# Softmax denominators written into a score bank of the next head pair

## Chip, cores and metric

The kernel runs on one core of one Trainium2 chip. The metric is the device time of one execution in microseconds. TensorE (PE) does matmuls and transposes, VectorE (DVE), ScalarE (ACT) and GpSimd (POOL) the rest, SyncE (SP) issues the DMAs. All of them run their own instruction lists in order and wait for each other by semaphores.

## What is computed

Attention with 4 sink keys and a window of 128 keys, for 4 batches of 8 heads with 768 queries of 64 numbers, and behind it a two-layer feed-forward net (512 to 2048 to 512, leaky ReLU) on the 3072 rows:

```python
scores = scale * np.matmul(q, k.transpose(0, 1, 3, 2))
keep = is_sink | in_window
scores = np.where(keep, scores, -1000000000.0)
scores = scores - np.max(scores, axis=-1, keepdims=True)
a = np.exp(scores)
a = a / (np.sum(a, axis=-1, keepdims=True) + 1e-09)
attn_out = np.matmul(a, v)
...
h = x @ w_in
g = np.maximum(0.01 * h, h)
return (g @ w_out).astype(np.float32)
```

All in float32. The feed-forward products are done in three passes on split operands.

## The kernel before

The work is cut into 8 units of 384 queries (half a batch), each of 4 pairs of heads and 3 query tiles (j = 0, 1, 2). A unit's attention gives the x of its feed-forward part, and one unit's feed-forward matmuls (16 steps, lines 549 and 586) are interleaved by hand on PE with the next unit's attention. Unit 0 has nothing to be interleaved with: its attention runs alone at the start of the program, with short dummy matmuls (line 272) between its transposes.

In units 0 and 1 ("native") one query tile of one pair goes as follows. PE computes the scores of the two heads into two PSUM banks (line 296; the two heads use different halves of PE's rows). DVE masks a bank and takes the row maximum (line 308), ACT does the exponential and the row sum into `sm` (line 310), POOL copies out the sink columns (line 458). Two tiles later PE transposes the result (line 337) and ACT (in pair 0 of unit 0: DVE) copies it to `pt` (line 342). When all three tiles of a pair are done, `spread` makes the reciprocals of the six row sums: DVE adds 1e-9 and writes the six numbers into columns of a score bank that the scores leave free (line 320, to `SPARE`, column 264 and up), takes the reciprocal from there back to `sm` (line 321), and POOL widens it to `rb` (line 324). `gather`, three tiles behind the pair's last one (two for the last pair of unit 0), transposes the sink columns and `rb` on PE (lines 372, 375) and copies them to `r` (line 379). `values`, one tile later, multiplies `pt` by the values (line 392) and the sinks (line 398), and DVE scales the result with `r` (line 404), which also frees the PSUM bank for a later transpose.

The score banks go round: four of them in unit 0 (tags s0, s1, o0, o1), two in unit 1 and later. A new score tile in a bank waits until the last instruction that reads or writes the old tile is done, and `spread`'s two DVE instructions count among these, since they use the bank's free columns. PE's order is written by hand (`attention_stream` with its lags, and `mlp_stream`). The orders on DVE, ACT, POOL and SP are set by a scheduler from the order in which the code emits the work. The same DVE also decodes the weights from 64-bit to 32-bit numbers (lines 185, 187, 189), and ACT and POOL split them (lines 198, 199); these lie between the attention's instructions all through units 0 and 1.

Of the kernel before, what the change touches and what calls it, by code (L numbers as in the profile page):

```python
# [147 lines left out]
def fast_path(ctx, tc, cpool, qp, qk, vu, vs, vt, wq, out, ident, lims, wz, negm, wmin, wmax):  # L148
# [68 lines left out]
    def native(u):  # L217
        return u < NATU

    def load_pair(u, pair):  # L220
        b, half = divmod(u, 2)
        n = TU + NK[half]
        raw = apool.tile([P, TU + NK[1]], F32, tag="qksp", name=f"qkn{u}_{pair}")
        nc.sync.dma_start(out=raw[:, 0:n], in_=qp[half][pair])
        raws[u, pair] = raw

    def load_values(u, pair):
        b, half = divmod(u, 2)
        vr = apool.tile([P, 4 * P], F32, tag="v", name=f"v{u}_{pair}")
        nc.sync.dma_start(out=vr[:, 0:NVB[half] * P], in_=vu[half][b, pair])  # L230
        vraws[u, pair] = vr

    def load_head(u, h):
        b, half = divmod(u, 2)
        n = TU + NK[half]
        raw = iopool.tile([P, TU + NK[1]], F32, tag="raw", name=f"qkraw{u}_{h}", bufs=3)
        nc.sync.dma_start(out=raw[:, 0:n], in_=qk[half][b, h])
        raws[u, h] = raw

    def load_sinks(u, pair):  # L240
        if native(u):
            sv = apool.tile([SKR, TU], F32, tag="sv", name=f"sv{u}_{pair}")
            nc.sync.dma_start(out=sv[0:SKN, :], in_=vs[u // 2, pair])
            svs[u, pair] = sv
            return
        raw = xpool.tile([SKR, TU], F32, tag="rb", name=f"svr{u}_{pair}", bufs=1)[:, 0:P]
        nc.sync.dma_start(out=raw, in_=vt[u // 2, pair])
        svs[u, pair] = raw
# [56 lines left out]
    def soft(u, h, j, w, src, mask, sm):  # L305
        col = (u * H + h) * T + j
        neg = negm[:, col:col + 1]
        anchor[0] = nc.vector.tensor_tensor_reduce(out=w, in0=src, in1=mask, scale=-SCALE, scalar=3.0e38,  # L308
                                                   op0=ALU.add, op1=ALU.min, accum_out=neg)
        nc.scalar.activation(out=w, in_=w, func=AF.Exp, scale=-1.0, bias=neg, accum_out=sm)  # L310
# [6 lines left out]
    def spread(u, pair, state, ps):  # L317
        sm = state["sm"]
        rest = ps[:, SPARE:SPARE + 2 * T].rearrange("p (j h) -> p j h", j=T)
        nc.vector.tensor_scalar(out=rest, in0=sm, scalar1=1e-9, scalar2=None, op0=ALU.add)  # L320
        nc.vector.reciprocal(out=sm, in_=rest)
        rb = xpool.tile([P, TU], F32, tag="rb", name=f"rb{u}_{pair}", bufs=1)
        rb = rb.rearrange("p (c d) -> p c d", c=2 * T)
        nc.gpsimd.tensor_copy(out=rb, in_=sm.rearrange("p j h -> p (j h)").rearrange("p (c o) -> p c o", o=1)
                              .broadcast_to([P, 2 * T, D]))
        state["rb"] = rb
# [89 lines left out]
    def ahead(u, pair):  # L416
        return (u, pair + 1) if pair < NPAIR - 1 else (u + 1, 0)

    count = [0]

    def attend(u, pair, pend):
        state = {"sk": sks[pair % 2]}
        nxt = ahead(u, pair)

        def later(lag, f, join=False):
            pend.append((count[0] + lag, f, join))

        def fetch(o):
            more = nxt[0] < NU
            if native(u) and native(nxt[0]) and nxt not in raws:  # L430
                load_pair(*nxt)
            if more and o == 0:
                load_values(*nxt)
            if not native(u) and o == 0:
                load_head(u, 2 * pair + 1)
            elif more and not native(nxt[0]):
                load_head(nxt[0], 2 * nxt[1])

        def tile_pt():
            if "pt" not in state:  # L440
                state["pt"] = apool.tile([P, 2, 2 * TU], F32, tag="pt", name=f"pt{u}_{pair}", bufs=1)

        def pt_then(f, *args):
            tile_pt()
            f(*args)

        if native(u):
            state["sm"] = apool.tile([P, T, 2], F32, tag="sm", name=f"sm{u}_{pair}")
            sp = raws.pop((u, pair))
            for j in range(T):  # L450
                kn = KSL[u % 2][j][1]
                pss = scores(u, pair, j, (0, 1), sp)
                w = apool.tile([P, 2, W3], F32, tag="pk", name=f"pk{u}_{pair}_{j}", bufs=3)
                a = P if kn == W3 else 0
                for o, ps in enumerate(pss):
                    soft(u, 2 * pair + o, j, w[:, o, 0:kn], ps[:, 0:kn], masks[min(T * (u % 2) + j, 2)],
                         state["sm"][:, j, o:o + 1])
                    nc.gpsimd.tensor_copy(out=state["sk"][:, 0, j, o, :], in_=w[:, o, a:a + NSK])
                if j == 0:
                    fetch(0)  # L460
                    if native(nxt[0]):
                        load_sinks(*nxt)
                    if u == 0 and pair == 0:
                        rest(anchor[0])
                    if u == 0 and pair == 2:
                        whole_lim.append(whole_limits(tc, cpool, lim_raw, lim_lo, anchor[0]))
                        late.append(late_masks(tc, cpool, iopool, masks, anchor[0]))
                count[0] += 1
                if j == T - 1:
                    spread(u, pair, state, pss[1])  # L470
                later(LAGT, lambda j=j, w=w: pt_then(turn_native, u, pair, j, w, state))
                yield
        else:
            for o in range(2):
                h = 2 * pair + o
                sp = split_head(u, h)
                fetch(o)
                (split_sinks if o else load_sinks)(u, pair)
                w = apool.tile([P, 2 * W3], F32, tag="pk", name=f"pk{u}_{h}", bufs=3)
                w = w[:, 0:T * W1].rearrange("p (j k) -> p j k", j=T)  # L480
                sm = apool.tile([P, T], F32, tag="sm", name=f"sm{u}_{h}")
                for j in range(T):
                    ps, = scores(u, pair, j, (o,), sp)
                    if KSL[u % 2][j][1] == W3:
                        nc.vector.copy_predicated(out=ps[:, W1:W3], mask=late[0][1], data=ps[:, 0:P])  # L485
                        src = ps[:, P:W3]
                    else:
                        src = ps[:, 0:W1]
                    soft(u, h, j, w[:, j], src, late[0][0][min(T * (u % 2) + j, 2)], sm[:, j:j + 1])
                    count[0] += 1  # L490
                    if j == T - 1:
                        nc.vector.tensor_scalar(out=sm, in0=sm, scalar1=1e-9, scalar2=None, op0=ALU.add)
                        nc.vector.reciprocal(out=sm, in_=sm)
                        nc.vector.tensor_tensor(out=w, in0=w, in1=sm.rearrange("p (j o) -> p j o", o=1)
                                                .broadcast_to([P, T, W1]), op=ALU.mult)
                        sk, sinks = state["sk"], w[:, :, 0:NSK]
                        nc.gpsimd.tensor_copy(out=sk[:, 0:3:2, 0:T, o, :].bitcast(F32R),
                                              in_=sinks.rearrange("p (r j) s -> p r j s", r=1)
                                              .broadcast_to([P, 2, T, NSK]))
                        nc.gpsimd.tensor_tensor(out=sk[:, 1, 0:T, o, :], in0=sinks, in1=sk[:, 0, 0:T, o, :],  # L500
                                                op=ALU.subtract)
                        later(LAGT, lambda o=o, w=w: pt_then(turn_packed, u, pair, o, w, state))
                    yield
        last = u == 0 and pair == NPAIR - 1
        if native(u):
            later(LAGT if last else LAGG, lambda: gather(u, pair, state))
        later(LAGT if last else LAGV if native(u) else LAGP, lambda: values(u, pair, state), not native(u))
# [125 lines left out]
    for x, _ in enumerate(mlp_stream()):  # L633
        u, r = divmod(x, mlp_steps)
# [216 lines left out]
```

## Time and profile before

| | |
|---|---|
| median of 3 runs | 702.59 us (701.48 to 704.52) |
| the profiled execution | 702.91 us, of which its span is 701.1 us |
| busy: PE, DVE, ACT, POOL | 98%, 64%, 45%, 46% of the span |
| granted TensorE clock, mean | 0.999 |

The span runs from the first to the last instruction; 1.8 us lie around it. PE is busy all the time but for the first 37 us or so, in which unit 0's attention runs alone, and for a few waits behind that. An engine that sits idle costs nothing unless PE waits for it.

### The profile page before, as it was taken

To read this page: it belongs to the slowest core of one execution; us is meant where nothing else is said; L and a number is where in the kernel's file an instruction comes from. 1 tells how busy PE (TensorE), PEld (TensorE's weight loads), DVE (VectorE), ACT (ScalarE), POOL (GpSimd) and SP (SyncE) were. 2 spreads that over 40 slices of the span, in tenths; PEclk is the share of its full clock that TensorE was granted. 3 is DMA by queue.
4 is the path that set the end of the run, shared out by engine and by line. 5 is a ranking of instruction groups with operands and counts; after the bars stand their busy time and mean duration, and the time that the engine had idled before them with its cause. 6 is when DMAs were issued, how large, how long until landed. Compare 5 with 4: busy or idle time off the path is not lost.

```text
span 701.1 us, 11524 instructions
## 1 busy us (share of the span) xinstructions
PE 687.3 (98%) x3950; PEld 597.8 (85%) x3950; DVE 446.1 (64%) x1183; ACT 318.8 (45%) x827; POOL 321.0 (46%) x442
## 2 busy tenths in 40 slices
PE   8899999999999999999999999999999999999996
PEld 5577788988888988888898888888888889889995
DVE  5997887655656665565566565556566565377772
ACT  4865566444454444444444444444444444222221
POOL 4676688544444543543444454354344444122220
PEclk9999999999999999999999999999999999999999
DMA  6666556222123111222113221221222320068751
GB/s 223 207 223 197 192 204 202 82 66 69 47 72 108 56 43 61 60 85 69 58 53 106 70 57 47 62 91 44 67 73 53 110 74 33 1 218 277 252 169 48
DMA packets 29535, 74.14 MB, mean 106 GB/s; under 512 B 3488, under 2 KB 9120, under 8 KB 29472
## 3 DMA queue, kind: packets, MB, share of 16 engines
q1 hardware_dynamic: 29184, 73.10, 32.0%
q8 instruction: 32, 0.52, 0.3%
q14 instruction: 31, 0.25, 0.1%
q10 hardware_dynamic: 288, 0.26, 0.1%
HBM read 67.06 MB, written 6.29 MB: 105 GB/s over the span
## 4 chain that ended last, share of the span: by engine, by line
PE 93%; DVE 3%; DMA 1%; ACT 1%; issue 0%; SPq 0%; ACTq 0%; DVEq 0%
PE h L549 38%; PE o L586 37%; PE acc L392 6%; PE s L301 5%; PE t L348 3%; PE s L296 2%; PE t L337 1%; DVE pk L308 1%; DMA qkraw<-in_qk 1%; PE acc L398 1%; DMA qkn<-in_qp 1%; PE acc L388 1%; PE t L350 0%; ACT pk L310 0%; DVE ob L599 0%
## 5 line engine op out<-in xcount | busy, mean ns | idle before, releaser
L568 POOL TENSOR_TENSOR gl<-g,gh 128x384 fp32r<-128x384 f32 x127 | 129.9, 1023 | 276.2 <-ACT gh L567 260.8
L549 PE MATMUL h<-xh,wih 128*128 128x384 f32 x512 | 180.8, 353 | 0.0
L549 PE MATMUL h<-xl,wih 128*128 128x384 f32 x512 | 172.7, 337 | 0.0
L549 PE MATMUL h<-xh,wil 128*128 128x384 f32 x512 | 172.7, 337 | 0.0
L586 PE MATMUL o<-woh,gh 128*128 128x512 f32 (+1 forms) x400 | 153.5, 385 | 0.2 <-DVE ob L599 0.2
L586 PE MATMUL o<-wol,gh 128*128 128x512 f32 (+1 forms) x400 | 152.8, 385 | 0.0
L310 ACT ACTIVATE pk<-pk,negm 128x132 f32<-128x132 f32 (+1 forms) x192 | 81.6, 426 | 96.7 <-DVE negm L308 96.3
L559 ACT ACTIVATE g<-h 128x384 f32<-128x384 f32 x127 | 62.0, 488 | 123.7 <-PE h L549 103.4
L586 PE MATMUL o<-woh,gl 128*128 128x512 f32 (+1 forms) x400 | 113.8, 387 | 0.0
L549 PEld LDWEIGHTS h<-xh,wih 128*128 128x128 f32 x512 | 96.4, 188 | 4.0 <-issue 2.2
L549 PEld LDWEIGHTS h<-xl,wih 128*128 128x128 f32 x512 | 96.6, 189 | 0.4 <-POOL xl L406 0.2
L549 PEld LDWEIGHTS h<-xh,wil 128*128 128x128 f32 x512 | 96.1, 188 | 0.0
L567 ACT CAST gh<-g 128x384 fp32r<-128x384 f32 x128 | 65.7, 513 | 65.4 <-DVE g L566 64.8
L566 DVE TENSOR_TENSOR g<-h,g 128x384 f32<-128x384 f32 x127 | 69.9, 550 | 35.0 <-ACT g L559 34.9
L586 PEld LDWEIGHTS o<-woh,gl 128*128 128x128 f32 x400 | 74.0, 188 | 17.1 <-POOL gl L568 0.4
L586 PEld LDWEIGHTS o<-woh,gh 128*128 128x128 f32 x400 | 75.1, 188 | 12.0 <-DVE ob L599 0.9
L586 PEld LDWEIGHTS o<-wol,gh 128*128 128x128 f32 x400 | 75.1, 188 | 11.0
L485 DVE COPY_PREDICATED s<-tri,s 128x128 f32<-128x128 int8 x120 | 35.0, 292 | 53.8 <-PE s L301 51.9
L262 POOL TENSOR_TENSOR qksp<-qkraw,qksp 64x396 fp32r<-64x396 f32 (+1 forms) x48 | 56.4, 1176 | 23.1 <-POOL gl L568 18.6
L301 PEld LDWEIGHTS s<-qksp 128*128 128x128 f32 x288 | 53.5, 188 | 8.6
L301 PE MATMUL s<-qksp 128*128 128x260 f32 (+1 forms) x288 | 56.3, 277 | 0.0
L261 ACT CAST qksp<-qkraw 128x780 fp32r<-128x780 f32 (+1 forms) x48 | 43.2, 901 | 25.2 <-PE s L301 22.2
(114 smaller groups left out, 853.8 us busy)
## 6 DMA issues: line engine op xcount, KB each, us to landing
craw<-in_wq SPq DMA_DIRECT2D x32, 512.0 KB, 4.1
qkraw<-in_qk SPq DMA_DIRECT2D x24, 454.0 KB, 3.2
qkraw<-in_qk SPq DMA_DIRECT2D x24, 390.0 KB, 3.0
wiraw<-in_wq SPq DMA_DIRECT2D x16, 512.0 KB, 4.2
woraw<-in_wq SPq DMA_DIRECT2D x16, 512.0 KB, 3.7
out<-ob SPq DMA_DIRECT2D x23, 256.0 KB, 2.0
v<-in_vu SPq DMA_DIRECT2D x16, 256.0 KB, 2.6
v<-in_vu SPq DMA_DIRECT2D x16, 192.0 KB, 2.4
```

The source lines that it names most:

```text
L261: nc.scalar.copy(out=sp[:, 0:TU + n], in_=raw[:, 0:TU + n])
L262: nc.gpsimd.tensor_tensor(out=sp[D:P, TU:TU + n], in0=raw[D:P, TU:TU + n], in1=sp[D:P, TU:TU + n].bitcast(F32), op=ALU.subtract)
L301: nc.tensor.matmul(pss[0][:, 0:kn], lhsT=sp[:, off + j * P:off + (j + 1) * P], rhs=sp[:, TU + k0:TU + k0 + kn], start=c == 0, stop=c == 1)
L310: nc.scalar.activation(out=w, in_=w, func=AF.Exp, scale=-1.0, bias=neg, accum_out=sm)
L392: nc.tensor.matmul(acc[o * D:(o + 1) * D, qo:qo + m], lhsT=vv[:, kb * P + o * D:kb * P + (o + 1) * D], rhs=state["pt"][:, o, po:po + m], s ...
L485: nc.vector.copy_predicated(out=ps[:, W1:W3], mask=late[0][1], data=ps[:, 0:P])
L549: nc.tensor.matmul(ph[:, 0:TU], lhsT=w[:, cs], rhs=x, start=cc == 0 and c == 0, stop=cc == NCC - 1 and c == 2)
L559: nc.scalar.mul(g, ph[:, 0:TU], 0.01)
L566: anchor[0] = nc.vector.tensor_tensor(out=g, in0=ph[:, 0:TU], in1=g, op=ALU.max)
L567: nc.scalar.copy(out=gh, in_=g)
L568: (nc.vector if step == NU * NFC - 1 else nc.gpsimd).tensor_tensor(out=gl, in0=g, in1=gh.bitcast(F32), op=ALU.subtract)
L586: nc.tensor.matmul(acc, lhsT=(gl if c == 2 else gh)[:, t * P:(t + 1) * P], rhs=(wl if c == 1 else wh)[:, cols], start=f == 0 and c == 0, s ...
```

## The change

`spread` of a pair is not emitted behind the pair's own last tile. It is kept in a list and emitted behind the two heads' line 308, 310 and 458 of the next pair's first tile, and the bank whose free columns it uses is that tile's second bank (`pss[1]`), not the second bank of the pair's own last tile. For the last pair of unit 1 it is the first bank of unit 2 (the second branch). Nothing is added or left out.

```diff
@@ in fast_path, ahead of attend @@
     count = [0]
+    waiting = []
...
@@ attend, units 0 and 1, in the loop over j @@
                 if j == 0:
+                    if waiting:
+                        waiting.pop()(pss[1])
                     fetch(0)
...
                 count[0] += 1
                 if j == T - 1:
-                    spread(u, pair, state, pss[1])
+                    waiting.append(lambda ps: spread(u, pair, state, ps))
...
@@ attend, the other units @@
                     soft(u, h, j, w[:, j], src, late[0][0][min(T * (u % 2) + j, 2)], sm[:, j:j + 1])
+                    if waiting:
+                        waiting.pop()(ps)
```

PE's order stays as it is. On the other engines the scheduler arranges the instructions anew. In the rows below, `s_5_0` is head 5's score bank of tile 0, and the number behind it only tells tiles of one name apart; `m` are masks, `di` and `wi` a weight being decoded, `lim` a small constant.

DVE, where pair 2 of unit 0 begins (the rows with `negm` alone read out the row maximum). Before:

```order
L185 TENSOR_SCALAR di_302<-wiraw_206 128x512
L107 SCALAR_TENSOR_TENSOR lim_hi<-lim_lo,lim_hi 128x2
L308 ISA pk_2_1_350,negm<-s_4_1_346,m_95 128x260
L308 ISA negm 128x1
L187 SCALAR_TENSOR_TENSOR di_302<-wiraw_206,di_302 128x512
L108 SCALAR_TENSOR_TENSOR lim<-lim_hi,lim_lo 128x2
L308 ISA pk_2_1_350,negm<-s_5_1_347,m_95 128x260
```

The same place now:

```order
L185 TENSOR_SCALAR di_302<-wiraw_206 128x512
L320 TENSOR_SCALAR s_5_0_255<-sm_1_184 128x6
L107 SCALAR_TENSOR_TENSOR lim_hi<-lim_lo,lim_hi 128x2
L308 ISA pk_2_1_350,negm<-s_4_1_346,m_95 128x260
L308 ISA negm 128x1
L187 SCALAR_TENSOR_TENSOR di_302<-wiraw_206,di_302 128x512
L308 ISA pk_2_1_350,negm<-s_5_1_347,m_95 128x260
L308 ISA negm 128x1
L321 RECIPROCAL sm_1_184<-s_5_0_255 128x6
L108 SCALAR_TENSOR_TENSOR lim<-lim_hi,lim_lo 128x2
```

Pair 1's lines 320 and 321, which stood ahead of line 404 of pair 0, have come behind it, line 321 behind both heads' line 308 of tile 1; they use bank `s_5_0`, which `s_5_2` needs next.

DVE, where unit 1 begins. Before:

```order
L320 TENSOR_SCALAR s_7_2_472<-sm_3_386 128x6
L321 RECIPROCAL sm_3_386<-s_7_2_472 128x6
L404 TENSOR_TENSOR r_2_491<-acc_2_520,r_2_491 128x384
L308 ISA pk_0_0_498,negm<-s_0_0_494,m_96 128x260
L308 ISA negm 128x1
L308 ISA pk_0_0_498,negm<-s_1_0_495,m_96 128x260
```

And now, from the last of these rows on:

```order
L308 ISA pk_0_0_494,negm<-s_1_0_491,m_96 128x260
L308 ISA negm 128x1
L185 TENSOR_SCALAR di_516<-wiraw_511 128x512
L320 TENSOR_SCALAR s_1_0_491<-sm_3_382 128x6
L308 ISA pk_0_1_555,negm<-s_0_1_551,m_96 128x260
L308 ISA negm 128x1
L187 SCALAR_TENSOR_TENSOR di_516<-wiraw_511,di_516 128x512
L321 RECIPROCAL sm_3_382<-s_1_0_491 128x6
```

Line 321 of pair 3 has moved behind unit 1's first bank of tile 1 and two weight steps, and the bank it uses, `s_1_0`, is the one of two that `s_1_1` needs next.

ACT, in pair 3 of unit 0. Before:

```order
L310 ACTIVATE pk_3_1_457,sm_3_386<-pk_3_1_457,negm 128x260 x2
L198 CAST wih_445<-wi_408 128x512
L379 COPY r_2_491<-sk_2_486 128x512
L310 ACTIVATE pk_3_2_475,sm_3_386<-pk_3_2_475,negm 128x260 x2
L198 CAST woh_449<-wo_413 128x512
```

And now:

```order
L310 ACTIVATE pk_3_1_457,sm_3_382<-pk_3_1_457,negm 128x260 x2
L198 CAST wih_445<-wi_408 128x512
L310 ACTIVATE pk_3_2_475,sm_3_382<-pk_3_2_475,negm 128x260 x2
L379 COPY r_2_487<-sk_2_482 128x512
L198 CAST woh_449<-wo_413 128x512
```

The copy of pair 2's gathered rows to `r` stands behind two exponentials that it stood ahead of.

## Rows read from the trace of the kernel before

**Rows 1.** Stretches: us, busy us of PE, PEld, DVE, ACT, POOL; clock, DMA, GB/s

```profile
9.50:36.70 27.20, 24.02 (x169) 14.97 (x168) 22.76 (x78) 19.89 (x63) 15.70 (x39) 1.00 0.60 203
40.00:60.00 20.00, 20.00 (x115) 15.34 (x113) 19.34 (x43) 12.97 (x32) 16.28 (x20) 1.00 0.69 220
36.70:700.50 663.80, 655.28 (x3743) 577.67 (x3741) 419.08 (x1083) 295.14 (x753) 300.22 (x376) 1.00 0.31 100
```

**Rows 2.** PE's waits in the first 30 us: us in total, times, longest

```profile
PE t L337 <- DVE r L404: 1.3, 2, 1.0
PE s L296 <- DVE sm L321: 0.9, 1, 0.9
```

**Rows 3.** Timeline, pair 1 of unit 0: start, us, engine, line, [idle before <-releaser]

```profile
9.54 0.70 PE L296 MATMUL s<-qkn 64*128 64x260 f32 x2
...
10.93 0.20 DVE L321 RECIPROCAL sm<-s 128x6 f32<-128x6 f32 x1
...
11.18 0.70 PE L296 MATMUL s<-qkn 64*128 64x260 f32 x2 [0.95 <-DVE sm L321]
11.82 0.66 PE L337 MATMUL t<-ident,pk 128*128 128x128 f32 x4
...
12.51 0.71 PE L296 MATMUL s<-qkn 64*128 64x260 f32 x4
...
13.74 0.30 PEld L296 LDWEIGHTS s<-qkn 64*128 64x128 f32 x4 [0.17 <-DMA qkn<-in_qp]
```

**Rows 4.** Timeline, pair 2 of unit 0

```profile
18.14 1.00 POOL L406 TENSOR_TENSOR xl<-r,xh 128x384 fp32r<-128x384 f32 x1
...
18.28 0.87 DVE L107 SCALAR_TENSOR_TENSOR lim_hi<-lim_lo,lim_hi 128x2 f32<-128x2 f32 x1
...
18.85 0.71 PE L296 MATMUL s<-qkn 64*128 64x260 f32 x4
...
20.02 0.15 DVE L108 SCALAR_TENSOR_TENSOR lim<-lim_hi,lim_lo 128x2 f32<-128x2 f32 x1
...
22.22 0.71 PE L398 MATMUL acc<-r,sv 32*128 32x128 f32 x4
```

**Rows 5.** Groups from 9 to 37 us: count | busy us, mean ns | idle before

```profile
L310 ACT ACTIVATE pk<-pk,negm 128x260 f32<-128x260 f32 x18 | 9.1, 509 | 3.3 <-DVE negm L308 3.1
...
L308 DVE CUSTOM_DVE_ANT_0 pk<-s,m 128x260 f32<-128x260 f32 x16 | 6.4, 422 | 1.4 <-PE s L296 1.3
...
L404 DVE TENSOR_TENSOR r<-acc,r 128x384 f32<-128x384 f32 x4 | 2.2, 545 | 2.4 <-PE acc L398 2.4
L187 DVE SCALAR_TENSOR_TENSOR di<-wiraw,di 128x512 int32<-128x512 int32 x3 | 2.1, 691 | 0.0
...
L324 POOL COPY rb<-sm 128x384 f32<-128x384 f32 x4 | 2.0, 505 | 0.9 <-PE t L337 0.4 <-PE acc L392 0.3 <-DVE sm L321 0.2
...
L379 ACT COPY r<-sk 128x512 f32<-128x512 f32 x3 | 1.7, 578 | 0.0
```

**Rows 6.** Timeline of PE, pairs 2 and 3 of unit 0 to the first h

```profile
24.46 0.66 PE L337 MATMUL t<-ident,pk 128*128 128x128 f32 x4 [1.05 <-DVE r L404]
...
31.07 0.66 PE L337 MATMUL t<-ident,pk 128*128 128x128 f32 x4 [0.30 <-DVE r L404]
...
31.77 0.71 PE L296 MATMUL s<-qkn 64*128 64x260 f32 x4
...
34.22 1.30 PE L392 MATMUL acc<-pt,v 128*64 128x256 f32 x12 [0.61 <-ACT pt L342]
...
36.73 0.44 PE L549 MATMUL h<-xh,wih 128*128 128x384 f32 x1
```

**Rows 7.** Timeline, unit 1, tiles 0 and 1 of pair 2

```profile
64.30 0.43 DVE L308 CUSTOM_DVE_ANT_0 pk<-s,m 128x260 f32<-128x260 f32 x1 [1.39 <-PE t L337]
64.65 0.42 DVE L308 CUSTOM_DVE_ANT_0 pk<-s,m 128x260 f32<-128x260 f32 x1
...
67.10 0.71 PE L296 MATMUL s<-qkn 64*128 64x260 f32 x4
```

## Prediction

> **What bounds the kernel now.** I read the stretches first: from 36.7 us to the end PE is busy 655.28 of 663.80 us, and the clock is 1.00 throughout [rows 1]. So behind 36.7 us nothing but PE's own work counts, and what the change can do it does by moving the first `h` matmul, at 36.73 [rows 6], and with it all that follows. Ahead of it PE is idle for about 3 of 27.2 us [rows 1]. The waits of PE come next: in the first 30 us it waits 0.9 us for line 321 and 1.3 us for line 404 [rows 2]. The first of these is the wait that the change is about: `s_3_1` (second head, tile 1 of pair 1) needs the bank of `s_1_2`, which pair 0's denominators hold until line 321 has ended at 11.13; it starts at 11.18 [rows 3]. It happens in one pair of the seven of units 0 and 1 that have one behind them. In the others the bank came free long before its next use.
>
> **Rules of the walk**, all from rows: a hand-over between engines takes 0.05 us (10.93 + 0.20 to 11.18), PE's next instruction starts about 0.06 before the end of the one ahead (11.18 + 0.70 to 11.82) [rows 3], DVE's about 0.08 before (64.30 + 0.43 to 64.65) [rows 7], unless it reads what that one wrote. The two heads' scores use different halves of PE's rows: both together take 0.71 us, one alone 0.70 [rows 3]. **So a wait that catches only the second head costs the wait and some 0.64 us more.** The added and removed instructions cancel: lines 320, 321 and 324 run as often as before; everything is in where they stand.
>
> **Pair 1: a gain that a transfer takes back.** `s_3_1` no longer waits, both heads go at 9.54, and the transpose behind them at 10.18 in place of 11.82 [rows 3]: 1.64 us gained. `s_2_2` follows 0.69 later, at 10.87 (11.82 to 12.51 before). But the denominators now sit in `s_3_0`, which `s_3_2` needs: DVE does line 320 and `s_3_1`'s line 308 and comes to line 321 at about 11.2, so `s_3_2` starts at 11.5 and ends its turn at 12.15. The gather (0.59 us) brings PE to 12.74. There it needs `qkn` of pair 2, whose transfer held it until 13.74 already, by 0.17 us [rows 3]; that transfer was issued much earlier and does not move. Gain: 0.
>
> **Pair 2: the new wait.** PE is unchanged up to `s_4_2` at 18.85 [rows 4]. On DVE line 320 slips in at about 18.3, ahead of line 107. Line 107 took 0.87 us and ended at 19.15, as POOL's line 406 ended (18.14 + 1.00); line 108, the same kind on as small a tile, took 0.15 [rows 4]. So line 107 waits for POOL, and line 320 hides in that. Line 308 of `s_5_1` takes line 108's place at 20.02, line 321 follows 0.35 later [rows 7], 20.37 to 20.57, and `s_5_2` can start at 20.62. `s_4_2` has run alone; PE gets on at 20.62 + 0.64 = 21.26, not at 19.49: 1.77 later. The copy to `rb` (0.51 [rows 5]) ends at 21.13 and is covered by that wait. Gather, `s_6_0` and `s_7_0` (0.59 + 0.42) and line 392 (1.30 less 0.06) bring line 398 to 23.50, against 22.22 [rows 4]: 1.28 later, since of the 1.77 a wait of 0.49 falls away, in which `s_7_0` stood for `s_5_1`'s line 308 (18.85 + 0.64 + 0.59 + 0.42 + 1.24 is 21.74, not 22.22). DVE has its weight steps done by about 23.9 and takes line 404 at 24.24, ends it at 24.79 (0.545 [rows 5]), and the transpose that needs its bank starts at 24.85. Before it stood there until 24.46, having waited 1.05 us for line 404 behind DVE's queue [rows 6]. So 0.39 is left of 1.28.
>
> A rule speaks against this place. The Trainium skill, page "SBUF — State Buffer", section "SBUF: two separate sides", says that VectorE and GpSimd share a pair of ports that one instruction holds to its end while the other is shut out, an instruction of VectorE with two inputs in SBUF being one that needs it. Line 107's 0.87 us agrees. By it the `rb` copy, which now comes right behind line 321, could shut out line 108 for 0.5 us; DVE would be free at 24.4 and the sum 0.2 larger. I leave it out, as line 108 starts about 0.1 us ahead of the copy.
>
> **Pair 3.** From line 404 at 24.24 DVE needs 2.24 us to line 321 (0.47, twice 0.22 for the narrow line 308, 0.61 each for lines 185 and 187, which is 0.69 less the overlap [rows 5], 0.12 for line 320): 26.48 to 26.66. PE, from 24.85, comes to `s_7_2` at 26.88. In time by 0.2 us, no wait. But on ACT the copy to `r` (line 379) now stands behind the two exponentials of tile 2 (0.51 each), the second of which can end at 29.97 only; the copy takes 0.58 [rows 5], so line 398 starts at 30.6 where PE is there at 29.97. Line 404 ends at 31.85 and the transpose behind it starts at 31.9, not at 31.07 [rows 6]: 0.83 later.
>
> **Unit 1, tiles 0 and 1.** Line 404 starts at 31.30, line 308 of the two banks of tile 0 at 31.74 and 32.09, line 185 at 32.44, line 320 at 33.04. Then stands line 308 of `s_0_1`, which PE runs alone from 32.60 to 33.30; then line 187 at 33.68 and line 321 from 34.28 to 34.46. Only two banks go round here, so `s_1_1` needs that one: it starts at 34.51, and the next transpose at 35.15, where before both heads went at 31.77 [rows 6] and it at 32.41. 2.74 later. `rb`, on POOL from about 34.5, is in time for the gather at 35.8. Line 342 then copies the transposes (35.85 to 36.42) and line 392 starts at 36.47, not at 34.22: 2.25 later, since 0.5 of the old wait of 0.61 [rows 6] is taken up. Behind it nothing waits, and the first `h` comes at 38.98 in place of 36.73.
>
> **In units 1 and 2** the new place is covered: in the tightest of the pairs, pair 2, line 308 of the second bank is at 64.65 [rows 7], lines 185, 320, 187 follow, line 321 would end at about 66.5, and the bank is wanted at 67.10 [rows 7]. If that cover is gone the cost is the lateness and 0.64.
>
> **The sum.** 0 + 0.39 + 0.44 + 1.42 = 2.25 us, on a span of 701.1: 703.35, and 705.16 for the execution with the 1.81 around it. The profiled execution was 0.32 above the median of 702.59, so the median becomes **704.8**. Bounds of the sum: if DVE kept the times of before up to pair 3's line 404, line 321 would still come a microsecond later than `s_1_1` is wanted, and the first `h` 1.1 us later: 703.7. If the 0.5 absorbed at 34.22 is not there and pair 3's margin of 0.2 fails: 2.25 + 0.5 + 0.3, 705.6.
>
> **Rivals.**
> 1. *The gain stays.* `qkn` lands earlier than the row shows, or the freed wait lets DVE run ahead so that none of the new places is late. For it: 1.64 us come free at 10.2 and DVE has nothing to do there. Against it: the transfer's wait at 13.74 [rows 3]. If all of the waits of [rows 2] go, 2.2 us: 700.4; if the new ones eat most of it, 702.6 to 703.
> 2. *Unit 1's two banks (slower).* Between 40 and 60 us DVE is busy 19.34 of 20 us and PE all of it [rows 1]. There line 321 holds a bank of two while DVE's queue is full. It decides from a lateness of 0.6 us on at 67.10 [rows 7]. At 2 us late that place costs 1.4 + 0.64, and PE has no idle time there to take it up: 702.6 + 2.25 + 2.0 = 706.9. Against it: DVE has 1.39 us of idle just ahead [rows 7], so its queue starts empty.
> 3. *The clock.* PE's pauses grow to about 1.3 us, twice. In the rows a pause of 1.05 us left the granted clock at 1.00 [rows 1, 6], its upper level of 2.4 GHz. If one of the new ones took it to 1.2 GHz, PE's work of 24.02 us in 27.2 [rows 1] would run at half speed in part: a quarter of it is 6 us, 708.6 or above. The Trainium skill, page "TensorE: Matmul & The Clock Gate", section "Part 1: The HAM clock gate", says that idleness halves the clock; no row here shows it.
> 4. *Nothing happens:* the wait for line 321 is only renamed and every new place is covered, 702.6. The order on DVE speaks against it.
>
> **How the numbers follow.** A measurement of this kernel can tell about 0.5% (3.5 us) from no change; 699.1 and 706.1 are the borders. My forecast, 0.58, with a range of 703.5 to 706.0. Rival 1, 0.15, and rival 4, 0.08, both mostly within 0.5%, with 0.03 of them faster. Rival 2, 0.14, and rival 3, 0.03, slower; 0.02 for other losses. A little of rival 2 stays within 0.5%. That gives faster 0.03, same 0.79, slower 0.18. The range of 701.8 to 706.9 takes in the forecast, rival 4, the upper half of rival 1 and the lower half of rival 2.
>
> **What would show it.** Right: PE's wait for line 321 ahead of `s_3_1` gone, and PE still waiting for `qkn` until about 13.7; new waits for line 321 of about 1 us at 20 to 21 us and at 33 to 35 us, each with one head's scores alone ahead of it; the first `h` near 39; behind it the same idle times as before. Wrong: the first `h` at or ahead of 36.7 (rival 1 or 4), waits of `s` for line 321 behind 40 us (rival 2), a granted clock below 1.00 in the first 40 us (rival 3).

## The result and the profile after

The changed kernel takes 709.02 us (707.67 to 709.51, 5 executions), against 702.59 (701.48 to 704.52) before: a ratio of 1.0079, 95% interval 1.0055 to 1.0103. The ratios here and below are worked out over the fast executions and are not quotients of two medians (709.02 by 702.59 is 1.0091); one execution of the kernel before, of 1356.57 us, counts nowhere. It is slower by 0.8%, where I had forecast 704.8 and at most 706.9. The profiled execution took 709.15 us, a span of 707.4 and 1.75 around it. The span is 6.3 us longer than the one of before.

The stretches come first again. These answer to [rows 1], with the same columns (us, busy us of PE, PEld, DVE, ACT, POOL; clock, DMA, GB/s):

```profile
9.50:41.70 32.20, 28.43 (x169) 17.19 (x168) 22.86 (x79) 20.40 (x64) 16.64 (x39) 0.88 0.52 184
20.00:24.00 4.00, 4.00 (x22) 2.47 (x21) 2.75 (x6) 2.66 (x7) 2.26 (x6) 0.57 0.68 234
36.90:43.90 7.00, 6.87 (x28) 4.83 (x28) 3.07 (x8) 2.74 (x9) 2.31 (x5) 0.52 0.48 162
41.70:706.80 665.10, 656.45 (x3743) 578.76 (x3741) 420.56 (x1082) 295.03 (x753) 298.62 (x375) 1.00 0.30 99
```

Behind the first `h` (now at 41.75) PE is idle 8.65 us, against 8.52 before: nothing new there. Ahead of it PE ran the same 169 matmuls, but was busy 28.43 us in place of 24.02. The reason stands in the clock's column: 1.00 over this whole part before, now 0.88, and 0.57 and 0.52 in two stretches. There PE runs at the lower of its two levels, 1.2 in place of 2.4 GHz.

PE's waits in the first 42 us (us in total, times, longest) answer to [rows 2]:

```profile
PE s L296 <- DVE sm L321: 1.3, 1, 1.3
...
PE s L296 <- ACT pt L342: 1.1, 1, 1.1
PE t L337 <- DVE r L404: 0.8, 3, 0.3
PE acc L398 <- ACT r L379: 0.4, 1, 0.4
```

The second of them is put down to line 342, since that ended last ahead of it, at 19.48. But line 342 copies transposes and touches no score bank; in the program `s_5_2` waits for one thing, line 321 on bank `s_5_0`. That ended at 19.42 (19.24 + 0.18; the row stands at the end of the section on the prediction), and `s_5_2` started at 19.49. So there are two waits of a second head for line 321, at the two places that the prediction names. The timeline of PE shows them and what followed (pair 1, then pair 2, then unit 1's first tiles; against [rows 3, 4, 6]):

```profile
9.49 0.71 PE L296 MATMUL s<-qkn 64*128 64x260 f32 x4
...
12.15 0.49 PE L375 MATMUL sk<-ident,rb 128*128 128x128 f32 x3
12.57 0.50 PE L296 MATMUL s<-qkn 64*128 64x132 f32 x4
...
17.68 0.70 PE L296 MATMUL s<-qkn 64*128 64x260 f32 x2
19.49 0.70 PE L296 MATMUL s<-qkn 64*128 64x260 f32 x2 [1.10 <-ACT pt L342]
20.12 0.48 PE L372 MATMUL sk<-ident,sk 128*128 128x128 f32 x1
20.39 0.85 PE L375 MATMUL sk<-ident,rb 128*128 128x128 f32 x3
...
21.91 2.06 PE L392 MATMUL acc<-pt,v 128*64 128x256 f32 x12
23.89 0.71 PE L398 MATMUL acc<-r,sv 32*128 32x128 f32 x4
...
33.09 0.70 PE L296 MATMUL s<-qkn 64*128 64x260 f32 x2
35.13 0.70 PE L296 MATMUL s<-qkn 64*128 64x260 f32 x2 [1.34 <-DVE sm L321]
...
37.10 2.40 PE L392 MATMUL acc<-pt,v 128*64 128x256 f32 x12
...
41.75 0.69 PE L554 MATMUL h<-xh,wih 128*128 128x384 f32 x1
...
44.94 0.60 PE L337 MATMUL t<-ident,pk 128*128 128x128 f32 x4
```

Each wait has one head's scores alone ahead of it (x2), then nothing, and each is followed within about 2 us by matmuls that take almost twice their time: line 375 0.85 in place of 0.49, line 392 2.06 and 2.40 in place of 1.30. So a pause of 1.10 and one of 1.34 us did what the pause of 1.05 had not done in the profiled execution of before [rows 6].

### The profile page after: what moved, and what is told of

The parts are those of the page before. It is cut to its first block, busy times and chain, and to the rows that moved or that the text cites. A ratio compares the mean times of both kernels' runs of the same rounds, so it can differ in the third digit from the quotient of the medians.

```text
span 707.4 us, 11538 instructions
## 1 busy us (share of the span) xinstructions
PE 692.9 (98%) x3950; PEld 601.1 (85%) x3950; DVE 447.8 (63%) x1183; ACT 319.2 (45%) x827; POOL 320.3 (45%) x442
## 4 chain that ended last, share of the span: by engine, by line
PE 93%; DVE 2%; ACT 1%; DMA 1%; POOL 0%; issue 0%; DVEq 0%; ACTq 0%; POOLq 0%
PE h L554 38%; PE o L591 36%; PE acc L392 6%; PE s L301 5%; PE t L348 3%; PE s L296 2%; PE t L337 1%; PE acc L398 1%; DMA wiraw<-in_wq 1%; DMA qkraw<-in_qk 1%; PE warm L272 1%; PE acc L388 0%; ACT pt L342 0%; PE t L350 0%; ACT pk L310 0%; DVE ob L604 0%
```

## The experiments

The theory was that the late line 321 costs what I had worked out, and that the rest is the clock, which falls behind a pause of PE. The rivals were that the waits themselves carry the whole loss, and that the clock falls for another reason. Twelve kernels ran, in four comparisons, each with the kernel before on the same chip. Every execution has a mean granted clock. In the six profiled ones in which no stretch ahead of 46 us lies below 1.00 it is 0.996 to 0.999, in those with such a stretch 0.989 to 0.995. The table counts the executions in which it was 0.995 or less.

| Kernel | Median us (executions) | Ratio to before, 95% | Clock 0.995 or less |
|---|---|---|---|
| before, all four comparisons | 703.45 (109) | | 56 |
| changed, the result above and a2_after | 709.10 (11) | 1.0079 and 1.0080 | 11 |
| e1_warm | 704.24 (12) | 1.0008 (0.9987 to 1.0028) | 1 |
| e1b_warm_boundary | 704.20 (12) | 1.0015 (0.9995 to 1.0034) | 3 |
| e2_not_boundary | 704.82 (12) | 1.0012 (0.9991 to 1.0033) | 6 |
| e3_only_boundary | 707.00 (12) | 1.0033 (1.0010 to 1.0056) | 12 |
| e6_pss0 | 706.93 (12) | 1.0044 (1.0022 to 1.0065) | 9 |
| e7_pair0 | 702.01 (12) | 0.9980 (0.9963 to 0.9997) | 0 |
| e8_before_warm | 702.03 (12) | 0.9973 (0.9953 to 0.9992) | 2 |
| e5_sbuf_old | 705.14 (12) | 1.0034 (1.0018 to 1.0050) | 1 |
| e9_pad64 | 705.78 (11) | 1.0040 (1.0021 to 1.0059) | 4 |
| e5c_sbuf_last | 702.45 (12) | 0.9985 (0.9971 to 0.9999) | 5 |
| e10_best | 702.08 (12) | 0.9980 (0.9960 to 1.0001) | 2 |

**Filling the pauses of the changed kernel.**

```diff
@@ scores, native units
             for o, ps in zip(heads, pss):
+                if o:
+                    keep_warm({(0, 2, 2): 6, (1, 0, 1): 12}.get((u, pair, j), 0))
                 rows = slice(o * D, (o + 1) * D)
```

> The changed kernel, with dummy matmuls (the warm ones of 256 columns, result unused) put on PE between the two heads' scores at the two places where the second head waits: 6 ahead of s_5_2, 12 ahead of s_1_1 of unit 1. The order on the other engines stays. Theory A (the pauses cost little themselves, but each is followed by PE at the lower granted clock): no stretch of the first 46 us below 1.00, line 392 at 37 us back from 2.40 to 1.30, the waits for line 321 as long as they were (now filled), first h near 39.0 in place of 41.75, time 704 to 705.5. Rival B (the time lies in the waits and in what they push, whatever the clock): the clock may rise, but first h stays above 41 and the time at 708.5 to 709.5. Rival C (the clock falls for another reason than the pause): clock still at 0.5 behind 20 and 37 us, time 709.

704.24: 4.8 us less than the changed kernel (which ran in other comparisons), though nothing was taken away and 18 matmuls were added. Its stretch ahead of the first `h` and its timeline (the lines are two higher here) show the same waits, filled, and the clock at 1.00:

```profile
9.50:39.20 29.70, 27.47 (x191) 17.11 (x189) 22.87 (x81) 20.59 (x65) 16.73 (x40) 1.00 0.60 203
```

```profile
18.84 0.70 PE L298 MATMUL s<-qkn 64*128 64x260 f32 x2
19.48 0.83 PE L272 MATMUL warm<-wz 128*128 128x256 bf16 x6
20.65 0.70 PE L298 MATMUL s<-qkn 64*128 64x260 f32 x2 [0.34 <-ACT pt L344]
...
23.53 0.71 PE L400 MATMUL acc<-r,sv 32*128 32x128 f32 x4
...
34.76 0.70 PE L298 MATMUL s<-qkn 64*128 64x260 f32 x2
...
36.73 1.30 PE L394 MATMUL acc<-pt,v 128*64 128x256 f32 x12
...
39.24 0.44 PE L556 MATMUL h<-xh,wih 128*128 128x384 f32 x1
...
41.48 0.60 PE L339 MATMUL t<-ident,pk 128*128 128x128 f32 x4
```

Both rivals fall: the waits are as late as they were (20.65 - 18.84 = 1.81, as 19.49 - 17.68), and without the pause there is no fall in the profiled execution and a low mean clock in only one of 12. The two falls can now be priced, each from the end of a wait to the same later matmul. From `s_5_2` to line 398: 4.40 us in the changed kernel, 2.88 here. From `s_1_1` to the transposes behind the first `h` group: 9.81 and 6.72. That is 1.52 + 3.09 = 4.6 us for these two executions, the 4.8 of the medians within 0.2.

With the dummies at the second place alone:

> The changed kernel with 12 dummy matmuls at the second place alone (ahead of s_1_1 of unit 1); s_5_2's pause is left as it is. Theory A (each pause makes its own fall of the clock): the first fall at 20 us stays in most executions, the second is gone; between e1 (704.2) and the changed kernel (709.0 to 709.6): 705 to 707, clocks of 0.993 to 0.998. Rival B (the first fall alone decides, and the second follows from it): both stay, 708 to 710.

704.20, under the range that I gave, but on theory A's side: 3 of 12 executions had a low clock. The profiled one (0.992, 707.17) is among them and shows the fall behind the first pause alone:

```profile
19.65 0.70 PE L298 MATMUL s<-qkn 64*128 64x260 f32 x2 [1.10 <-ACT pt L344]
...
21.30 2.33 PE L394 MATMUL acc<-pt,v 128*64 128x256 f32 x12
...
38.51 1.30 PE L394 MATMUL acc<-pt,v 128*64 128x256 f32 x12
```

The other nine have mean clocks of 0.996 to 0.998, so the fall did not stay "in most executions", as I had it. The second pause does most of the harm.

**Taking the change apart.**

```diff
@@ e2_not_boundary, against the changed kernel
                 if j == T - 1:
-                    waiting.append(lambda ps: spread(u, pair, state, ps))
+                    if u == 0 and pair == NPAIR - 1:
+                        spread(u, pair, state, pss[1])
+                    else:
+                        waiting.append(lambda ps: spread(u, pair, state, ps))
```

> The changed kernel, but the last pair of unit 0 writes its denominators into its own last bank, as before the change; the other pairs as changed. Theory A: s_1_1 of unit 1 goes together with s_0_1, no second fall of the clock; the first one (20 to 24 us) stays with s_5_2's wait. First h at 37.5 to 38.1, time 703.4 to 704.2. Rival B (the loss comes from pair 2 and is only carried on to 42 us): first h above 40, time 707 to 709.

704.82, 0.6 above what I gave. Its profiled execution has no second fall and the first `h` at 38.09, as theory A says. Half of its executions have a low mean clock, the profiled one among them, whose fall is the first one (line 392 behind `s_5_2` takes 2.40); where the others fell is not known. That would put the median between.

```diff
@@ e3_only_boundary, the same place
-                    waiting.append(lambda ps: spread(u, pair, state, ps))
+                    if u == 0 and pair == NPAIR - 1:
+                        waiting.append(lambda ps: spread(u, pair, state, ps))
+                    else:
+                        spread(u, pair, state, pss[1])
```

> The kernel before, with the change at one place alone: the denominators of unit 0's last pair go into the first bank of unit 1's pair 0. Theory A: up to 31 us as before, s_1_1 waits about 1 us for line 321 and some 2.7 us of lateness follow, then PE at the lower clock for some 6 us: first h 41 to 42, time 707 to 708. If the wait comes without a fall of the clock: first h 39, time 704.5 to 705. Rival B (the loss is made in pair 2): time 702.6 to 703.5. The times of e2 and e3 above the kernel before should add to the 6.4 us of the whole change if the two places act by themselves.

707.00: 3.6 us above the kernel before beside it, e2 1.5 above. That is 5.1 of the 5.6 to 6.4 of the whole change. All 12 executions had a low clock. Its trace held a surprise: up to 31 us the order is that of the kernel before, and yet the clock falls there too, right behind the wait that the change was to remove (stretches of e3, then its timeline):

```profile
10.00:12.00 2.00, 1.05 (x5) 0.55 (x5) 1.07 (x6) 1.31 (x6) 1.17 (x5) 1.00 0.84 338
12.50:15.50 3.00, 3.00 (x15) 1.77 (x16) 2.24 (x7) 1.53 (x6) 0.51 (x3) 0.51 0.26 53
```

```profile
9.46 0.70 PE L296 MATMUL s<-qkn 64*128 64x260 f32 x2
11.12 0.70 PE L296 MATMUL s<-qkn 64*128 64x260 f32 x2 [0.95 <-DVE sm L321]
...
13.79 0.85 PE L375 MATMUL sk<-ident,rb 128*128 128x128 f32 x3
```

The same rows with the same 0.95 us stand in [rows 3]. There line 375 behind them took 0.49:

```profile
13.32 0.49 PE L375 MATMUL sk<-ident,rb 128*128 128x128 f32 x3
13.74 0.49 PE L296 MATMUL s<-qkn 64*128 64x132 f32 x4
```

So whether the clock falls behind a given pause differs from one execution to the next, and the kernel before has such a pause too. Two runs tested that. e7 is e3 with another condition:

```diff
-                    if u == 0 and pair == NPAIR - 1:
+                    if (u, pair) == (0, 0):
```

> The kernel before, with the change for pair 0 alone: its denominators go into the first bank of pair 1, all other pairs as before. s_3_1 then no longer waits for line 321. By the prediction's step (pair 2's qkn lands at 13.74 whatever PE does) nothing is gained: 702.4 to 702.8, with PE waiting at s_4_0 for qkn. By the trace of the changed kernel, where s_4_0 started at 12.57 without a wait: PE and DVE both run 1.2 us earlier from there, first h at 35.5, time 701.2 to 701.6.

702.01, between the two. In 12 executions it took 701.22 to 703.07, none with a low clock: `s_3_1`'s pause is gone, and so is the spread of the kernel before (700.72 to 708.30 over all comparisons). No matmul was added here, so a pause taken away does what dummies in a pause do. The wait of 1.05 us for line 404 is still there, with no low clock in any of the 12:

```profile
23.88 0.66 PE L337 MATMUL t<-ident,pk 128*128 128x128 f32 x4 [1.05 <-DVE r L404]
...
36.14 0.44 PE L557 MATMUL h<-xh,wih 128*128 128x384 f32 x1
```

```diff
@@ e8_before_warm: the kernel before, scores
             for o, ps in zip(heads, pss):
+                if o:
+                    keep_warm(6 if (u, pair, j) == (0, 1, 1) else 0)
                 rows = slice(o * D, (o + 1) * D)
```

> The kernel before, with 6 dummy matmuls on PE between s_2_1 and s_3_1 of pair 1, where s_3_1 waits 0.95 us for line 321; nothing else moves. Theory A (a pause on PE lets the clock fall in some executions and not in others, and the kernel before has one such pause): the executions of the kernel before reach from 701.2 to 708.3 us with mean clocks of 0.987 to 0.999; with the dummies they lie between 701 and 704 with clocks of 0.996 or more, median 702.2 to 702.8, s_3_1 as late as it was. Rival B (the spread of the kernel before comes from elsewhere, for instance the transfers at the start): the spread stays, to 706 or more, with clocks below 0.994.

702.03 (700.78 to 703.72), a little better than I gave, and 0.27% below the kernel before with an interval of 0.08 to 0.47%; two executions had 0.994 and 0.995 all the same. `s_3_1` starts as late as it did, its pause now 0.18:

```profile
9.54 0.70 PE L298 MATMUL s<-qkn 64*128 64x260 f32 x2
11.19 0.70 PE L298 MATMUL s<-qkn 64*128 64x260 f32 x2 [0.18 <-DVE sm L323]
...
13.33 0.49 PE L377 MATMUL sk<-ident,rb 128*128 128x128 f32 x3
13.75 0.30 PEld L298 LDWEIGHTS s<-qkn 64*128 64x128 f32 x4 [0.17 <-issue]
13.75 0.50 PE L298 MATMUL s<-qkn 64*128 64x132 f32 x4
```

So six dummies get back some 1.8 us of the kernel before's 703.8 beside it, and nothing but PE's pause was touched. Not all of it shows in the mean clock: of the executions with 0.997 or more, those of e8 have a median of 701.80, those of the kernel before beside it 702.49. Rival B falls, and theory A holds for both kernels, but for the two low executions that it had not allowed.

**One head ahead of the pause, or none.**

```diff
@@ e6_pss0, native branch
-                        waiting.pop()(pss[1])
+                        waiting.pop()(pss[0])
```

> The changed kernel, with the denominators in the first head's score bank of the next pair in place of the second's. Then the first head waits for line 321 and the second stands behind it: PE idles all of the lateness in one piece (about 1.8 us at s_4_2, 2.0 at unit 1's s_0_1) in place of 1.1 and 1.3 with one head's scores ahead. Theory A (the loss is the lateness plus the clock): PE is free behind the pair of heads at the same time as in the changed kernel (20.1 and 35.8 us, less or more 0.3), the clock falls in all executions, time 708.5 to 711. Rival B (one head alone, at half of the array, is what costs): 0.6 us less at each place, 707 to 708.

706.93: below the ranges of both.

```profile
19.55 0.84 PE L296 MATMUL s<-qkn 64*128 64x260 f32 x4 [1.73 <-DVE lim L108]
20.32 0.47 PE L372 MATMUL sk<-ident,sk 128*128 128x128 f32 x1
```

It is not rival B's reason that makes it so: PE is free at the same time (the gather at 20.32, against 20.12), and nothing of the 0.6 us is gained. What differs is that 3 of the 12 executions had no low clock (703.63 to 704.81) and the rest up to 709.75. Beside it:

> The changed kernel again, beside the other three on one chip, for more executions of it. Theory A: two pauses, each of which lets the clock fall in most executions: clocks of 0.988 to 0.996, 706 to 710, with the fastest of the executions (no fall) near 704; ratio to the kernel before 1.006 to 1.009. Rival B (it falls always and by the same length): 708 to 710, no execution below 707.

709.62 (706.63 to 710.62, 6 executions), ratio 1.0080 (1.0051 to 1.0108), all with a clock of 0.987 to 0.993: the first result again. Neither 'most executions' nor an execution near 704 came; rival B missed too, since its lowest is 706.63. By the table, kernels with a pause of 1.34 us behind one head's scores had a low clock in every execution (changed kernel, e3), those with 1.10 us alone in part of them (e1b, e2), e6 with 1.73 and 1.36 us and no head ahead not in all, and e7 with 1.05 us for line 404 in none. So the length of a pause alone doesn't decide; what does, stays open.

**No bank at all.** If the bank's hold makes the wait, a tile in SBUF ends it.

```diff
@@ e5_sbuf_old, spread, the kernel before
-        rest = ps[:, SPARE:SPARE + 2 * T].rearrange("p (j h) -> p j h", j=T)
+        rest = xpool.tile([P, T, 2], F32, tag="rest", name=f"rest{u}_{pair}")
```

> The kernel before, with the denominators in a small SBUF tile and no bank held; POOL's and ACT's order stays, line 321 of pair 0 moves behind line 308 of s_3_1 as in e7. Theory A (what waits is the bank): no wait of PE for line 321 and no pause of that kind, 701.3 to 702.3, clocks of 0.996 or more, like e7 (702.0). Rival B (holding the bank was not what s_3_1 waited for, or writing to SBUF costs DVE more next to POOL): line 320 or 321 above 0.4 us, time 703 or more.

Neither. The wait was gone and the first `h` came at 35.83, 0.9 earlier than before, with the clock at 1.00. Yet it took 705.14. The loss lay behind 36 us, spread over the feed-forward matmuls. The tile had moved the tiles behind it up by 64 bytes (`r`, `xh`, `xl`, `g`, `gh`, `gl` and the buffers of `iopool`; the split weights stand ahead of it), and two runs settled that this was it:

```diff
@@ e9_pad64: the kernel before, and an unused tile at that place
         nc.gpsimd.memset(sks[i], 0.0)
+    nc.gpsimd.memset(xpool.tile([P, 2 * T], F32, tag="rest", name="pad"), 0.0)
```

> The kernel before, with an unused tile of 2 x 24 bytes a partition put where e5 had its tile (one memset on POOL at the start): all tiles behind it stand 64 bytes higher, nothing else changes. Theory A of e5c: 2.5 to 3 us slower than the kernel before for an equal clock, 705 to 706.5, with 575 matmuls in 100 us. Rival B: as the kernel before, 703.4 to 703.8.

705.78, theory A. Its stretch behind the first `h` reads against the last of [rows 1]:

```profile
36.60:703.10 666.50, 658.33 (x3743) 579.42 (x3741) 419.60 (x1083) 294.97 (x753) 299.31 (x376) 1.00 0.31 100
```

The same 3743 matmuls keep PE busy 658.33 in place of 655.28 us, at the same granted clock. In e5c the small tile stands in `iopool`, the last pool, so that only that pool's buffers move:

```diff
-        rest = xpool.tile([P, T, 2], F32, tag="rest", name=f"rest{u}_{pair}")
+        rest = iopool.tile([P, T, 2], F32, tag="rest", name=f"rest{u}_{pair}")
```

> As e5 (the kernel before, denominators in a small SBUF tile), but the tile stands in the last pool of SBUF, so that the operands of the MLP's matmuls keep their addresses; in e5 they stood 64 bytes higher, and every h and o matmul behind 36 us ran about half a per cent slower (575 in place of 580 in 100 us), though its first h came 0.9 us earlier than in the kernel before. Theory A (the addresses made e5's loss): 580 matmuls in 100 us, first h at 35.8, 701 to 702, clocks of 0.996 or more. Rival B (the loss comes from writing the denominators to SBUF, or from the order behind 36 us): 704.5 to 705.5, as e5.

702.45; its executions with a clock of 0.996 or more took 701.0 to 702.6, as theory A says. But five of 12 had a low one, and in the profiled execution it falls behind a wait of 1.23 us for line 404, not line 321 (clock 0.80 from 23 to 25 us, 0.50 from 25 to 27):

```profile
23.56 0.66 PE L337 MATMUL t<-ident,pk 128*128 128x128 f32 x4 [1.23 <-DVE r L404]
24.26 1.24 PE L296 MATMUL s<-qkn 64*128 64x260 f32 x4
```

So I filled that one too, behind the transposes of `t_2_0`:

```diff
@@ e10_best, turn_native, against e5c
         if u == 0:
-            keep_warm(1)
+            keep_warm(7 if (pair, j) == (2, 0) else 1)
```

> e5c (the kernel before, denominators in a small SBUF tile at the end of SBUF) with 6 more dummy matmuls behind the transposes of t_2_0, where PE then waits 1.23 us for line 404 and where e5c's profiled execution shows the clock at 0.50 right behind. Theory A (a pause lets the clock fall, whatever it waits for): of e5c's 12 executions 5 had a clock of 0.995 or less; with the dummies at most 2 have, median 701.3 to 702.1, below both kernels. Rival B (only the pauses for line 321, with one head's scores ahead, do it): the clocks as in e5c, median 702.3 to 702.7.

702.08, two executions with a low clock, as theory A has it. By counts of 2 and 5 in 12 alone the theories are not told apart, but the profiled execution helps, one of the two (705.46 us, 0.993). It shows a third sort of pause, for a transfer, and matmuls at the lower clock right behind it. No bank and no line 321 is waited for there:

```profile
11.59 0.55 PE L375 MATMUL sk<-ident,rb 128*128 128x128 f32 x3
13.71 0.50 PE L296 MATMUL s<-qkn 64*128 64x132 f32 x4 [1.57 <-DMA qkn<-in_qp]
14.13 2.03 PE L392 MATMUL acc<-pt,v 128*64 128x256 f32 x12
```

e7, e8, e5c and e10 have ratios to the kernel before of 0.9973 to 0.9985, that is 0.15 to 0.27% below it (e10's interval just reaches 1.0001); which of them is best these intervals don't tell.

## Why the prediction was wrong, and where it was right

**The walk was right.** e1_warm is the changed kernel with the clock held, and in its profiled execution `qkn` came as late as I had assumed. That is luck: in the changed kernel's it came 1.2 us earlier. Start of each step in us:

| Step | Predicted | e1_warm | Changed kernel |
|---|---|---|---|
| pair 2's first scores, `s_4_0` | 13.74 | 13.73 | 12.57 |
| `s_5_2`, behind line 321 | 20.62 | 20.65 | 19.49 |
| line 398 of pair 2 | 23.50 | 23.53 | 23.89 |
| line 398 of pair 3 | 30.6 | 30.59 | 30.96 |
| `s_1_1` of unit 1, behind line 321 | 34.51 | 34.76 | 35.13 |
| line 392 behind it | 36.47 | 36.73 | 37.10 |
| first `h` | 38.98 | 39.24 | 41.75 |
| the execution | 705.16 | 705.23 | 709.15 |

So the new waits, the 0.64 us that a second head left alone costs, the copy to `r` behind two exponentials, and what each of them absorbs came out within 0.3 us.

**The step that failed is the clock's term, which the sum left at nothing.** Rival 3 named it, I gave it a chance of 0.03, and my reason was that "a pause of 1.05 us left the granted clock at 1.00". That was one row of one execution. Over 109 executions of that same kernel 56 had a low clock, with times to 708.30; the 45 with 0.997 or more have a median of 702.52. In the changed kernel there were two such pauses, 1.10 and 1.34 us long, where I had taken one of 0.95 away, and behind both the clock fell to the lower level: 4.6 us, where the sum has 0. Rival 3's own price, "a quarter of it is 6 us", was a guess at a share and no working from rows; that its 708.6 lies near 709.02 is luck, since it adds 6 us to the kernel before without the sum's 2.25. The prediction's range ended 1.7 us below that price and so left it out.

The Trainium skill, page "TensorE: Matmul & The Clock Gate", section "A second HAM failure mode: psum-queue depth-cycling", describes another kernel, whose matmul groups go round through banks of PSUM, and in which PE's frequent short idle times between the groups make the clock go down and up. These runs agree in part: waits of 0.95 to 1.34 us for a bank, and 0.51 to 0.57 granted behind them, but here a single wait was followed by a fall, and waits for a transfer or for line 404 were too. I had cited the page for its general rule alone.

**Pair 1's gain was misread.** That "a transfer takes back" the gain rested on the 0.17 us of [rows 3]. That is the wait of the weight load, not of PE. In e8 the same 0.17 stands at the same place and is put down to "issue" (above), and PE goes from line 375 to `s_4_0` in 0.42 us in both (13.32 to 13.74 before, 13.33 to 13.75 in e8). The row didn't tell when `qkn` had landed. The row of its issue does (KB, us from issue to landing; issued at 7.30 in the profiled execution of before, at 7.26 in that of the changed kernel):

```profile
qkn<-in_qp SPq DMA_DIRECT2D x1, 390.0 KB, 6.2
...
qkn<-in_qp SPq DMA_DIRECT2D x1, 390.0 KB, 5.1
```

By it, as an estimate, `qkn` landed at about 13.5 before and 12.4 in the changed kernel. So a gain of 0 was nearly right for the one execution that I had read, by the wrong row, and what was wrong was that the transfer "does not move": over the kernels here it takes 4.9 to 6.6 us. The gain is 1.17 us in some executions, as in the changed kernel's, and 0 in others, as in e1's. In e7's profiled execution the first `h` comes at 36.14, 0.59 earlier than before. What it is worth in the median the runs don't tell: e7's 702.01 is 0.5 us below the executions of before without a low clock, but e8, which takes no wait away, is 0.7 below its own by the same measure.

**The sum by medians.** Executions with a clock of 0.997 or more: 702.52 before, 703.83 in e1 (10 of them). By these the late line 321 costs 1.3 us net, where I had 2.25 with no gain in pair 1. Against e8, the kernel before with its own pause filled, it is 2.2 (704.24 and 702.03, from two comparisons). The profiled e1, without the gain of pair 1, has its first `h` 2.5 us later than before. The clock's part is 4.8 to 5.4 us on top for the changed kernel, and 0.9 (by these executions) to 1.8 (by e8) for the one before.

**Rival 2** didn't come: behind 42 us PE waits 1.9 us for line 342 (2.0 before), and nowhere for line 321. **Rivals 1 and 4** fall with the two waits, though rival 1's condition came in part: in the changed kernel `qkn` did land earlier. The rule on the shared ports, which I left out, had no effect: line 108 was done ahead of the copy to `rb` (which starts at 19.56) in 0.11 us:

```profile
19.24 0.18 DVE L321 RECIPROCAL sm<-s 128x6 f32<-128x6 f32 x1
19.35 0.11 DVE L108 SCALAR_TENSOR_TENSOR lim<-lim_hi,lim_lo 128x2 f32<-128x2 f32 x1
```

## What to carry to other kernels

A change that moves a wait is to be priced with the clock in mind: here the new pauses cost 1.3 to 2.2 us net by themselves, and 1.5 and 3.1 us more where the clock fell behind them. Whether it falls differs between executions of one program, so a profile without a fall doesn't show that a pause is harmless; a wide spread of the times, and the mean clock of each execution, show it. Where a pause couldn't be removed, a few dummy matmuls in it were nearly free here: with six of them `s_3_1` started at 11.19 in place of 11.18.

## What the runs showed that I had not expected

- Six dummy matmuls in one pause of the kernel before make it 0.27% faster (0.08 to 0.47%), and its spread falls from 7 us (29 executions) to 3 (12).
- Moving operands up by 64 bytes in SBUF, with not one instruction of PE changed, costs 2.4 us of the median (e9 against before, 705.78 and 703.34), and 3.05 us of PE's busy time behind the first `h`. Per matmul that is 1 to 2 ns (the `o` products from `gh` 396 in place of 394 ns). What in the addresses does it was not tried.
- The same transfer of 390 KB, issued at 6.9 to 7.8 us in each kernel, took between 4.9 and 6.6 us to land.
